# Score products of batches 3 to 7 by row-tiled matmuls, v products pair by pair from batch 4 on, and attention's ranks moved forward, in a block-causal attention and SwiGLU kernel

## Chip, cores and metric

The kernel runs on one core of a Trainium2 chip. The metric is the device time of one launch in microseconds (us), as the median of several runs. Five engines work side by side: TensorE (PE, with its weight loads shown apart as PEld), VectorE (DVE), ScalarE (ACT), GpSimd (POOL) and SyncE (SP, which here issues nearly all DMAs).

## The reference, cut to what matters

```python
# q, k, v: (8 batches, 8 heads, 576 positions, 64), fp32; q and k scaled up by about 4
scores = (1.0 / np.sqrt(64)) * np.matmul(q, k.transpose(0, 1, 3, 2))
mask   = (pos // 64)[:, None] >= (pos // 64)[None, :]          # causal by blocks of 64
scores = np.where(mask, scores, -1e9)
attn   = np.exp(scores - scores.max(-1, keepdims=True))
attn   = attn / (attn.sum(-1, keepdims=True) + 1e-09)
x      = np.matmul(attn, v)                                    # -> (4608 tokens, 512)
g      = x @ w_gate                                            # 512 -> 1536
out    = (g / (1 + np.exp(-g)) * (x @ w_val)) @ w_out          # 1536 -> 512
```

Tokens are numbered batch by batch, so that batch b gives tokens 576 b to 576 b + 575.

## The kernel before, in words

**Precision.** Wherever fp32 accuracy is wanted, an operand is kept as two fp32r parts, "high" (a rounded copy, made by ACT) and "low" (what the copy lost, made by DVE), and a product is made of three: high by high, high by low, low by high.

**Attention.** `attention(...)` (L358) lists the work of one pair of heads of one batch; there are four pairs in a batch, 32 in all. It computes scores transposed (128 keys on the partitions, queries along the row) for the five chunks of keys of a head, only for the queries that may see the chunk, so the chunks are 576, 448, 320, 192 and 64 queries wide. Then: maxima over chunks (DVE, L721) and over partitions (POOL, L725), subtraction (DVE, L749), exponent (ACT, L753), products with v (PE, L831, 28 matmuls for a pair, two heads side by side in the 64-column halves), sums over chunks (DVE, L721 again) and over partitions (POOL, L882), and stores of x and of the sums to DRAM (SP, L900 and L907). There are three ways of making the scores, chosen by batch at L706:

- `plain_scores` (batches 0 and 1): plain fp32 products, L453.
- `split_scores` (batches 3 to 7, 20 pairs): for each head, high and low part of the keys lie one above the other on all 128 partitions, so that two matmuls with 128 rows (L580) make the three products: 24 matmuls for a pair. They come in four groups (two for each head), each with a PSUM buffer `at` of its own, of which there are two. Before them, for q and for k: a load (4 DMAs, L527), a transpose (DVE, L538), three copies in 64-partition halves (ACT, L542; two of them for k) and two subtractions in halves (DVE, L548). Behind them: four copies out of PSUM (ACT, L590) and six small ones that hide the blocks not to be seen (ACT, L600).
- `row_scores` (batch 2, in the set `ROWS`, 4 pairs): the heads lie in the two 64-row halves of the array, and a matmul of 64 rows of one head is issued next to that of the other; three matmuls for a chunk and head (L664), 36 for a pair. They come in four groups too (288 queries, 288 queries, 448 + 64, 320 + 192), each with an `at`. Before them, for q and for k: the same 4 DMAs and transpose (L640), one copy (ACT, L643) and one subtraction (DVE, L646) on 128 partitions. Behind them: four copies out of PSUM (ACT, L681) and three that hide (ACT, L693).

**Products with v.** A pair's generator stops where its products with v are to be made, and is kept in the list `at_work`. `with_v(rank)` (L1248) makes one task of all pairs in the list: of one pair in batches 0 and 1, of two pairs from batch 2 on (one run of 56 matmuls).

**SwiGLU.** `feed_forward(j, ...)` (L1077) does tile j of 256 tokens, 18 tiles. Each has six steps: 24 matmuls for gate and 24 for value (both L1116, PSUM buffers `gv`), tanh (ACT, L1150), two multiplications (DVE, L1153 and L1158), high part (ACT, L1163), low part (DVE, L1166), and 12 matmuls with w_out (L1208, L1209, L1210). In tiles 0 to 3 (`FINE`) these are cut into small tasks; from tile 4 on the 48 matmuls of gate and value follow each other without anything between, and the 12 are one task.

**Order of the work.** All tasks are put in a list with an engine, an estimated cost, a rank, predecessors and buffers. `in_order()` (L1305) plays the engines through with these costs: an engine that comes free takes, among the tasks whose predecessors are done and whose buffers are free, that of lowest rank; PE prefers a task of the same `mode` as the last ("rows" for the 64-row products, "columns" for the products with v). The program is then issued in that order, for every engine and for the queues of SP and POOL. Buffers of `qk`, `parts`, `sc`, `mx`, `v`, `xu`, `gv`, `hhl` and others are handed out in order of creation (`IN_TURN`), and most of them there are two of; a pair from batch 2 on holds one `sc` (scores), one `mx`, one `v` and one `xu`.

The rank of a pair h of batch b is, from batch 2 on, `10 + b - LEAD + h/8`, with corrections `SHIFT` for batches 2 and 3; its scores up to the maxima have a rank lower by `EAGER`. The ranks of SwiGLU's matmuls are `10 + token/576` from tile 2 on (10.89 and up), of its ACT and DVE work 0.5 and a little, of fetching x 1.0 and a little. Pieces of the weights, which are taken apart by ACT and DVE at the beginning, have ranks of -47 to 60. Where the plan leaves PE idle for over 0.3 us, small matmuls on ones (L1425) fill the gap.

Of the kernel before, what the change touches and what calls it, by code (L numbers as in the profile page):

```python
# [18 lines left out]
def kernel(  # L19
# [30 lines left out]
    XT = 256  # L50


    LEAD, EAGER = 6.5924, 0.1229

    SUMS = 2


    ROWS = (2,)
    MIXED = (0, 0, 1, 1, 0, 1, 0, 0, 1, 1, 0, 1)

    FINE = 4
# [296 lines left out]
    def attention(R, b, h, a, e, early, bufs, lane):  # L358
# [346 lines left out]

        (plain_scores if early else row_scores if b in ROWS else split_scores)()  # L706

# [538 lines left out]
    at_work = []  # L1246

    def with_v(rank):  # L1248
        us, products, after, bufs = zip(*(next(pair) for pair in at_work))
        t = add(  # L1250
            "PE", sum(us), rank, lambda: [f() for f in products], sum(after, []), sum(bufs, []), mode="columns"
        )
        for pair in at_work:
            try:
                pair.send(t)
            except StopIteration:
                pass
        at_work.clear()
# [3 lines left out]
    for b in range(B):  # L1262
        for a, e, R in FIRST.get(b, [(0, S, 10.0 + b - LEAD)]):
            early = b in FIRST
            lanes = 2 if e <= half else 1
            for h in range(0, H, 2):
                lane = h // 2 % lanes
                if not lane:
                    if early:
                        bufs = [Buf("qk", "pair"), Buf("parts", "pair")]  # L1270
                    elif b in ROWS:
                        bufs = [(Buf("qk", "raw"), Buf("qk", "keys")), Buf("parts", "queries")]
                    else:
                        bufs = [
                            (Buf("qk", "raw"), Buf("qk", "high")),
                            (Buf("parts", "low0"), Buf("parts", "low1")),
                        ]
                    bufs += [Buf(x) for x in "sc mx v xu".split()]
                    bufs.append(Buf("sr") if b < SUMS else bufs[3])
                rank = R[h // 2] if early else R + h / H + (SHIFT[b][h // 2] if b in SHIFT else 0.0)  # L1280
                at_work.append(attention(rank, b, h, a, e, early, bufs, lane))

                if early or len(at_work) == 2:
                    with_v(rank)
    for i in range(NFC):
        for kind in range(3):
# [174 lines left out]
```

## Time and profile before

| | |
|---|---|
| median of 3 runs | 1163.17 us (1162.48 to 1164.80) |
| span of the profiled execution, first to last instruction (what lies around it isn't listed apart) | 1161.9 us |
| PE busy | 1149.6 us |
| DVE, ACT, POOL busy | 742.4, 620.0, 321.0 us |
| granted TensorE clock, mean | 0.997 |
| bytes moved by DMA | 197.44 MB, mean 170 GB/s |
| first and last matmul of L664 (batch 2) | 205.2 and 271.4 us |
| first and last matmul of L580 (batches 3 to 7) | 303.9 and 903.3 us |

In the lists of the timeline, a row gives the start, the duration, engine, line and operation, what it writes and reads, its shape, and how many equal ones follow each other (x24). Matmuls overlap each other in these durations; what one costs is the distance from its start to the next one's start. A table by stretches gives the busy time of every engine in each stretch, the number of instructions (x), the granted clock as a share (PEclk), and the share and rate of the DMA engines.

### The profile page before, as it was taken

Reading aid. Unit: us, or ns where it says so; the run is one execution under the profiler, and the core shown is the slowest. Engines: PE = TensorE matmul, PEld = TensorE weight load, DVE = VectorE, ACT = ScalarE, POOL = GpSimd, SP = SyncE. Lnnn points to the kernel's source line nnn. Section 1 sums busy time; section 2 is a strip of 40 time slices with the busy share of each in tenths; the row PEclk is TensorE's granted clock in tenths of the full one; section 3 lists DMA queues with packets and bytes.
Section 4 is the critical chain, followed back from the end, with each engine's and each line's share of the span. In section 5 each row is a group of like instructions: output and inputs, shape, how many; then the busy total and the mean of one; then the engine's idle time right before and its main releaser. Section 6 shows DMA issues by size and latency. Waiting matters only on the chain.

```text
span 1161.9 us, 22310 instructions
## 1 busy us (share of the span) xinstructions
PE 1149.6 (99%) x8744; PEld 1032.7 (89%) x8744; DVE 742.4 (64%) x1230; ACT 620.0 (53%) x1114; POOL 321.0 (28%) x141
## 2 busy tenths in 40 slices
PE   8999999999999999999999999999999999999998
PEld 6678788889899989898998989898998989999997
DVE  4998898877697857576774747576575643323222
ACT  5889776745676655473745556473655422212111
POOL 3213101153525263334133423333233420000000
PEclk8999999999999999999999999999999999999999
DMA  8757757776657466663656565663674445444442
GB/s 204 211 158 211 201 190 237 200 206 159 169 149 204 117 188 180 193 152 115 188 169 198 140 185 143 196 166 121 173 201 150 144 144 172 144 164 138 144 170 103
DMA packets 266986, 197.44 MB, mean 170 GB/s; under 512 B 195264, under 2 KB 231376, under 8 KB 266880
## 3 DMA queue, kind: packets, MB, share of 16 engines
q1 hardware_dynamic: 264304, 195.29, 58.0%
q8 instruction: 69, 1.13, 0.4%
q10 hardware_dynamic: 2576, 0.72, 0.3%
q14 instruction: 37, 0.30, 0.1%
HBM read 171.57 MB, written 24.38 MB: 169 GB/s over the span
## 4 chain that ended last, share of the span: by engine, by line
PE 92%; ACT 4%; DMA 2%; DVE 1%; SPq 0%; issue 0%; ACTq 0%
PE gv L1116 50%; PE at L831 8%; PE po L1208 8%; PE po L1210 7%; PE po L1209 7%; PE at L580 6%; PE at L453 1%; PE at L664 1%; PE at L1208 1%; PE at L1209 1%; PE at L1210 1%; ACT sc L471 1%; DMA qk<-in_k_dram 1%; ACT sc L753 1%; PE at L427 0%; ACT ob L970 0%
## 5 line engine op out<-in xcount | busy, mean ns | idle before, releaser
L1116 PE MATMUL gv<-xhl,v_all 128*128 128x256 f32 x2592 | 323.4, 278 | 0.1
L1116 PEld LDWEIGHTS gv<-xhl,v_all 128*128 128x128 f32 x2592 | 308.1, 188 | 4.0 <-issue 1.5
L725 POOL PARTITION_ALL_REDUCE mx<-mx x80 | 140.6, 1805 | 391.5 <-DVE mx L721 138.8
L882 POOL PARTITION_ALL_REDUCE mx<-mx x48 | 178.2, 3765 | 227.0 <-DVE mx L721 213.5
L1153 DVE SCALAR_TENSOR_TENSOR t<-t,gv 128x512 f32<-128x512 f32 x108 | 73.9, 684 | 159.8 <-ACT t L1150 159.1
L1116 PE MATMUL gv<-xhl,g_even 128*128 128x256 f32 x1296 | 173.4, 280 | 0.0
L1116 PEld LDWEIGHTS gv<-xhl,g_even 128*128 128x128 f32 x1296 | 164.2, 188 | 7.0 <-issue 0.8
L1116 PE MATMUL gv<-xhl,g_odd 128*128 128x256 f32 x1296 | 168.9, 277 | 0.0
L1116 PEld LDWEIGHTS gv<-xhl,g_odd 128*128 128x128 f32 x1296 | 157.1, 188 | 1.9 <-issue 1.4
L1163 ACT CAST hhl<-t 128x512 fp32r<-128x512 f32 x108 | 67.2, 622 | 164.3 <-PE po L1209 88.4
L1208 PE MATMUL po<-wo,hhl 128*128 128x512 f32 x372 | 147.5, 397 | 0.0
L1210 PE MATMUL po<-wo,hhl 128*128 128x512 f32 x372 | 145.2, 390 | 0.4 <-DVE hhl L1166 0.4
L1209 PE MATMUL po<-wo,hhl 128*128 128x512 f32 x372 | 145.5, 391 | 0.0
L1166 DVE TENSOR_TENSOR hhl<-t,hhl 128x512 fp32r<-128x512 f32 x108 | 83.3, 773 | 89.5 <-ACT hhl L1163 89.2
L749 DVE TENSOR_TENSOR sc<-sc,mx 128x640 f32<-128x640 f32 (+6 forms) x168 | 122.8, 772 | 16.9 <-POOL mx L725 16.8
L1150 ACT ACTIVATE t<-gv 128x512 f32<-128x512 f32 x108 | 64.6, 598 | 114.9 <-PE gv L1116 109.6
L1158 DVE SCALAR_TENSOR_TENSOR t<-t,gv 128x512 f32<-128x512 f32 x108 | 73.8, 683 | 80.1 <-PE gv L1116 79.2
L753 ACT ACTIVATE sc<-sc 128x1024 f32<-128x1024 f32 (+3 forms) x104 | 105.6, 1031 | 33.7 <-DVE sc L749 33.1
L721 DVE TENSOR_TENSOR mx<-mx,sc 128x128 f32<-128x128 f32 (+2 forms) x180 | 105.0, 588 | 2.2
L590 ACT ACTIVATE sc<-at 128x576 f32<-128x576 f32 x80 | 66.8, 838 | 52.6 <-PE at L580 51.0
L831 PE MATMUL at<-sc,v 128*64 128x320 f32 (+4 forms) x888 | 91.5, 359 | 1.2 <-ACT parts L435 0.9
L831 PEld LDWEIGHTS at<-sc,v 128*64 128x64 f32 x888 | 58.9, 137 | 35.1 <-issue 2.1
(161 smaller groups left out, 1409.2 us busy)
## 6 DMA issues: line engine op xcount, KB each, us to landing
wo<-wo_d SPq DMA_DIRECT2D x200, 512.0 KB
out_dram<-ob SPq DMA_DIRECT2D x35, 256.0 KB
v<-in_v_dram SPq DMA_DIRECT2D x64, 128.0 KB
xt<-x_d SPq DMA_DIRECT2D x64, 128.0 KB
rt<-r_d SPq DMA_DIRECT2D x128, 64.0 KB
qk<-in_q_dram SPq DMA_DIRECT2D x112, 72.0 KB
qk<-in_k_dram SPq DMA_DIRECT2D x104, 72.0 KB
x_d<-xu SPq DMA_DIRECT2D x24, 288.0 KB
```

The costliest lines, as they stand in the source:

```text
L721: nc.vector.tensor_tensor(into, prev, of(c), op)
L725: nc.gpsimd.partition_all_reduce(m, m, channels=P, reduce_op=bass_isa.ReduceOp.max)
L749: nc.vector.tensor_tensor(piece(c), scores_of(c), m, ALU.subtract)
L753: nc.scalar.activation(x, x, AF.Exp)
L831: nc.tensor.matmul(ps[0][own(x), 1 - i if sums else i, q0 - s0 : s1 - s0], lhsT=ones if sums else vt[0][:, 2 * lane + c, own(x)], rhs=sc[0 ...
L882: nc.gpsimd.partition_all_reduce(m, m, channels=P, reduce_op=bass_isa.ReduceOp.add)
L1116: nc.tensor.matmul(o, lhsT=part[:, d], rhs=xs[d][1][x][:, 0:w], start=first, stop=last)
L1153: nc.vector.scalar_tensor_tensor(t[0][:, 0:n], t[0][:, 0:n], 1.0, pg[0][:, 0:n], ALU.add, ALU.mult)
L1166: nc.vector.tensor_tensor(hh[1][:, 0:n], t[0][:, 0:n], hh[0][:, 0:n].bitcast(F32), ALU.subtract)
L1208: nc.tensor.matmul(po, lhsT=hi, rhs=whi, start=i + y == 0, stop=False)
L1209: nc.tensor.matmul(po, lhsT=hi, rhs=wlo, start=False, stop=False)
L1210: nc.tensor.matmul(po, lhsT=lo, rhs=whi, start=False, stop=i + y == NFC - 1)
```

## The change

The ranks of attention from batch 2 on become lower by 3.41 (10.0 instead of 6.5924 is taken off), `EAGER` changes from 0.1229 to 0.1; the scores of batches 3 to 7 are made by `row_scores` instead of `split_scores`; and from batch 4 on `with_v` is called for each pair alone, where batches 2 and 3 keep two pairs together.

```diff
-    LEAD, EAGER = 6.5924, 0.1229
+    LEAD, EAGER = 10.0, 0.1
...
-    ROWS = (2,)
+    ROWS = (2, 3, 4, 5, 6, 7)
...
                 at_work.append(attention(rank, b, h, a, e, early, bufs, lane))

-                if early or len(at_work) == 2:
+                if early or len(at_work) == (2 if b < 4 else 1):
                     with_v(rank)
```

## The prediction

> **What bounds the kernel now.** I read the page first (busy time of the engines), then a table by stretches, then PE's timeline around the runs of attention's matmuls, then the groups of DVE, ACT and POOL.
>
> ```profile
> span 1161.9 us, 22310 instructions
> PE 1149.6 (99%) x8744; PEld 1032.7 (89%) x8744; DVE 742.4 (64%) x1230; ACT 620.0 (53%) x1114; POOL 321.0 (28%) x141
> 200.00:300.00 100.00, 99.64 (x778) 87.97 (x779) 81.44 (x127) 61.92 (x105) 31.68 (x13) 1.00 0.70 192
> 300.00:940.00 640.00, 640.00 (x4808) 585.38 (x4805) 430.12 (x674) 360.35 (x647) 244.62 (x84) 1.00 0.58 165
> 940.00:1162.00 222.00, 218.23 (x1582) 204.28 (x1580) 63.84 (x109) 40.78 (x74) 2.11 (x1) 1.00 0.45 149
> ```
>
> PE is busy for 1149.6 of 1161.9 us, and from 300 to 940 us for all of it, at a clock of 1.00, while DVE has 430 of 640 us, ACT 360, POOL 245. From 300 us on nothing but PE's own work sets the end: SwiGLU's matmuls fill every gap that attention leaves, and attention ends before 940, with 222 us of SwiGLU alone behind it. From 200 to 300 us PE lacks 0.4 us; the 3.8 us missing at the end are the last tile's way out. So the change is worth what it does to the sum of PE's matmuls and of the distances between them. The other engines count only where they would leave PE without work.
>
> **Scores, batches 3 to 7 (20 pairs).** What a matmul costs is the distance between starts. First SwiGLU alone, as a measure; then a pair of batch 2 (`row_scores`), whose four groups go in two visits, with the work before and behind each; then the visits of another pair of it that stayed single.
>
> ```profile
> 958.41 2.88 PE L1116 MATMUL gv<-xhl,v_all 128*128 128x256 f32 x24
> 961.13 0.40 PE L1208 MATMUL po<-wo,hhl 128*128 128x512 f32 x1
> ...
> 265.66 1.18 PE L1116 MATMUL gv<-xhl,g_odd 128*128 128x256 f32 x9
> 266.77 1.06 PE L664 MATMUL at<-parts,qk 64*128 64x288 f32 x12
> 267.76 0.62 PE L1116 MATMUL gv<-xhl,g_odd 128*128 128x256 f32 x3
> 268.22 0.39 PE L1208 MATMUL po<-wo,hhl 128*128 128x512 f32 x1
> ...
> 269.37 0.40 PE L1210 MATMUL po<-wo,hhl 128*128 128x512 f32 x1
> 269.70 1.97 PE L664 MATMUL at<-parts,qk 64*128 64x448 f32 x24
> 271.60 0.50 PE L1208 MATMUL po<-wo,hhl 128*128 128x512 f32 x1
> 271.94 0.40 PE L1209 MATMUL po<-wo,hhl 128*128 128x512 f32 x1
> ...
> 204.74 0.50 PE L1116 MATMUL gv<-xhl,g_even 128*128 128x256 f32 x3
> 205.17 0.67 PE L664 MATMUL at<-parts,qk 64*128 64x288 f32 x6
> 205.76 0.62 PE L1116 MATMUL gv<-xhl,g_even 128*128 128x256 f32 x3
> 206.22 0.87 PE L1116 MATMUL gv<-xhl,v_all 128*128 128x256 f32 x6
> ```
>
> 24 products of L1116 take 961.13 - 958.41 = 2.72, so one takes 0.113 and three take 0.34; one of L1208 to L1210 takes 0.23 where nothing disturbs it (684.33 - 684.10 in the next fence). The visit of 12 (288 and 288 queries) lasts from 266.77 to 267.76, 0.99. The nine products ahead of it take 1.11 instead of 1.02 (+0.09), the three behind it 0.46 instead of 0.34 (+0.12): 1.20 in all. The visit of 24 lasts from 269.70 to 271.60, 1.90; ahead of it L1210 takes 0.33 instead of 0.23 (+0.10), behind it L1208 takes 0.34 (+0.11): 2.11. **A pair in two visits costs 3.31.** Each visit pays some 0.21 for the change into 64-row tiles and back. The price of a visit that breaks up follows from the last four rows: a single group of 288 lasts 0.59 and pays 0.09 and 0.12, 0.80, so two of them 1.60 instead of 1.20, +0.40. The other half pays at least for coming and going once more, +0.21. I take the mean, 0.3; a pair in four visits costs 3.31 + 0.61 = 3.92.
>
> Now `split_scores`, which the change takes away:
>
> ```profile
> 684.10 0.39 PE L1210 MATMUL po<-wo,hhl 128*128 128x512 f32 x1
> 684.33 0.29 PE L580 MATMUL at<-qk,parts 128*128 128x288 f32 x1
> ...
> 685.97 0.41 PE L1208 MATMUL po<-wo,hhl 128*128 128x512 f32 x1
> 686.22 0.39 PE L1209 MATMUL po<-wo,hhl 128*128 128x512 f32 x1
> ...
> 705.72 0.30 PE L580 MATMUL at<-qk,parts 128*128 128x288 f32 x1
> ...
> 707.38 0.41 PE L1208 MATMUL po<-wo,hhl 128*128 128x512 f32 x1
> ...
> L580 PE MATMUL at<-qk,parts x240: 191/292/471, 303.9 to 903.2; 128*128 128x288 f32 x40, 128*128 128x448 f32 x40, 128*128 128x320 f32 x40
> L664 PE MATMUL at<-parts,qk x144: 188/292/469, 205.2 to 271.4; 64*128 64x288 f32 x48, 64*128 64x448 f32 x24, 64*128 64x64 f32 x24, 64*128 64x320 f32 x24
> ```
>
> A run of 12 lasts from 684.33 to 685.97, 1.64, and from 705.72 to 707.38, 1.66. Ahead of it L1210 takes its usual 0.23; behind it L1208 takes 0.25 (+0.02). Full-height matmuls come and go almost without a price. **A pair costs 3.34.** The 240 matmuls of this row, from 303.9 to 903.2, alternate with as many on the low queries; the 480 lie in 44 runs: 36 of 12, four of 4 and four of 8; a broken run costs nothing here. Of the 144 of L664 the first two pairs went in eight visits and the last two in four.
>
> So the new scores have less work inside the visits (0.99 + 1.90 = 2.89 against 3.30) and give nearly all of it back in coming and going, the doors of a visit. In two visits each: 20 x (3.31 - 3.34) = -0.6 us. In four visits each: 20 x (3.92 - 3.34) = +11.6. These are the bounds. I take two visits for all but one half of the 40: from batch 4 on SwiGLU's tasks between two visits are 12 to 48 matmuls long, and between the visits ACT has only two copies of 576 to make where it has 576 and 1024 today, under which 36 of 40 halves held together. That adds one break, +0.3.
>
> The Trainium skill, TensorEngine Tiling (Array Packing), Key Properties, says that changing the tiling mode drains the TensorE, without a figure; the trace agrees, 0.09 to 0.12 us each way. The Trainium skill, same title, Theoretical Speedup, promises up to 2x where the contraction is 64 or less; what that would make stands with the third rival.
>
> The loads stay (4 DMAs for q and 4 for k on SP in both forms), as do the transposes, POOL's work and the number of `at` buffers. ACT and DVE get less work for each pair:
>
> ```profile
> L548 DVE TENSOR_TENSOR parts<-sr,qk 64x576 fp32r<-64x576 f32 x38 | 28.5, 750 | 8.4 <-ACT qk L542 8.0
> L646 DVE TENSOR_TENSOR qk<-sr,qk 128x576 fp32r<-128x576 f32 x4 | 3.0, 750 | 0.0
> L749 DVE TENSOR_TENSOR sc<-sc,mx 128x1152 f32<-128x1152 f32 (+4 forms) x100 | 77.5, 816 | 15.7 <-POOL mx L725 15.7
> ```
>
> DVE makes two subtractions of 0.75 for four, -1.5 a pair; ACT two casts for six and three hiding copies for six. I cost that at nothing: PE hides it, and it is worth at most the 0.4 us that PE lacks from 200 to 300 us.
>
> **Products with v alone, batches 4 to 7 (16 pairs).** Eight visits become 16. What a further visit costs:
>
> ```profile
> 673.10 2.88 PE L1116 MATMUL gv<-xhl,v_all 128*128 128x256 f32 x24
> ...
> 675.91 2.92 PE L831 MATMUL at<-sc,v 128*64 128x256 f32 x28
> ...
> 678.66 2.88 PE L831 MATMUL at<-sc,v 128*64 128x256 f32 x28
> 681.47 0.50 PE L1208 MATMUL po<-wo,hhl 128*128 128x512 f32 x1
> 681.81 0.39 PE L1209 MATMUL po<-wo,hhl 128*128 128x512 f32 x1
> ```
>
> This run of 56 holds two pairs (shown in its halves, from two windows). The 24 products ahead of it take 2.81 instead of 2.72, +0.09. Its first half takes 2.75, its second, which ends in the change back, 2.81, +0.06. L1208 behind it takes 0.34, +0.11. Together 0.26, and 8 x 0.26 = +2.1 us; the other bound is 0, if two pairs come ready so close that the plan puts them side by side. I take +2.1: the pairs come one by one.
>
> Today a couple's first pair waits with its products, and holds its `sc`, `v` and `xu`, until its partner's exponents are done. Alone, it leaves earlier, and the pair after next gets these buffers earlier: attention runs faster and ends well before 940 us. That moves SwiGLU's matmuls, and makes none shorter. In PE's queue the run of 28 waits for one pair's exponents instead of two; what stands behind it is SwiGLU, whose next step the plan puts ahead where the exponents come later.
>
> **Ranks.** All pairs from batch 2 on move by the same 3.41, so their order among themselves stays; `EAGER` moves no pair past another. Buffers go in order of creation, so no pair of batch 2 can pass the last one of batch 1 (rank 29.1), on SP's queue or POOL's either, and the first 200 us stay. On PE, batch 2's first pair (12.88 to 9.47) and batch 3's third (11.87 to 8.46) pass tiles 2 and 3 (10.89 to 11.78); the others were ahead already. On DVE, ACT and SP three pairs pass SwiGLU's 0.5 and the 1.0 of fetching x: batch 2's fourth (1.62 to -1.79) and batch 3's second and fourth. There a block of five subtractions, 5 x 0.816 = 4.1 us, can go ahead of a step's tanh, products or low part. Bounds: 0, and 3 x 4.1 = 12.2 us if PE had nothing else. The nearest row is the stretch from 300 to 940 us, where PE is full beside 430 us of DVE. I take +0.2. Below nothing is excluded but for the 0.4 us that PE lacks there.
>
> **Sum.** -0.6 + 0.3 + 2.1 + 0.2 = +2.0 us on a span of 1161.9: 1163.9. The median of the runs lies 1.27 above that span, so the time is 1163.17 + 2.0 = 1165.2 us. Less than 0.2% (2.3 us) is about what a measurement of this kernel, whose three runs spread over 2.3 us, can't tell from no change.
>
> **Rivals.** (1) *The visits break up*, which ends slower. `at` has two buffers, and a visit of two groups needs both when PE turns to it. Now single v runs, twice as many, hold one at other times than the scores' own. For it: batch 2's first two pairs all went in single groups. Against: its last two didn't, nor did 36 of 40 halves of the split form. It decides from a second and third break on (1.7 + 3 x 0.3 = 2.6, over the 2.3); ten, one in every other pair, give 1163.17 + 1.7 + 3.0 = 1167.9.
>
> (2) *SwiGLU is fed late* by the three pairs that overtake it, or by DVE and POOL in a denser attention. For it: DVE has 81 of 100 us from 200 to 300, where PE lacks 0.4. Against: PE lacks nothing at 67% of DVE later. Half of the 12.2 gives 1163.17 + 1.8 + 6.1 = 1171.1; it decides from 0.5 us on.
>
> (3) *The tiles pay*, which ends faster: if score visits and v visits come side by side, the doors vanish, 20 x (2.89 - 3.34) = -9.0, and with the eight v visits 1163.17 - 9.0 + 2.1 = 1156.3. Against: none of the rows above has such a neighbour. If two heads in half the rows cost one, 36 matmuls would be 18 full ones against 24, 3.30 x 18/24 = 2.48 a pair: 1163.17 + 20 x (2.48 - 3.34) + 2.1 gives 1148.1; the 2.89 measured inside is against it, and it has 0.01 of this rival's chance. The Trainium skill's 2x (TensorEngine Tiling (Array Packing), Theoretical Speedup) is this case.
>
> (4) *The change does less than it says*: the v runs meet and stay in couples. Then 1163.17 - 0.6 + 0.3 + 0.2 = 1163.1.
>
> **How the numbers follow.** The forecast 0.52, of which 0.15 lie over the border of +2.3 us (its own range is 1164 to 1167); rival (1) 0.17, (2) 0.13, (3) 0.12, (4) 0.06. Faster: (3), 0.12. Same: 0.37 + 0.06 = 0.43. Slower: 0.15 + 0.17 + 0.13 = 0.45. The range leaves out most of (3) and the upper part of (1) and (2), some 0.2: 1161.5 to 1169.5.
>
> **What the profile after would show.** L580 gone and 864 matmuls of L664, in 40 to 45 visits from batch 3 on; 16 runs of 28 and four of 56 of L831 from batch 2 on; PE at 100% from 300 us on; DVE busy for some 30 us less (20 x 1.5), ACT for more than that; POOL idle well before 940 us. PE's busy time higher by about 2 us. The prediction is wrong if visits of single groups are common, if PE shows gaps between 200 and 400 us, or if visits of L664 and L831 stand side by side.

## The result, and the profile after

The changed kernel takes 1171.07 us (median; 1169.60 to 1172.78) against 1163.36 of the kernel before in the same series: a ratio of 1.0065 [1.0053, 1.0077], +7.7 us. In a second series (e11 below) it was 1.0046 [1.0032, 1.0060], +6.1 us. It is slower than the 1165.2 forecast and lies above the range of 1161.5 to 1169.5; of the rivals it is (2), SwiGLU fed late, that shows in the trace. The profiled execution took 1169.60 us, its span is 1167.8.

The page of the kernel after, its first two lines of numbers:

```profile
span 1167.8 us, 22687 instructions
PE 1154.6 (99%) x9024; PEld 1024.6 (88%) x9024; DVE 714.4 (61%) x1186; ACT 549.0 (47%) x974; POOL 316.3 (27%) x141
```

The table by stretches of the kernel after (PE, PEld, DVE, ACT, POOL busy; PEclk; share and rate of DMA):

```profile
200.00:300.00 100.00, 99.18 (x755) 87.88 (x754) 72.27 (x116) 56.95 (x98) 32.26 (x13) 1.00 0.66 184
300.00:940.00 640.00, 639.68 (x5068) 570.99 (x5067) 411.01 (x644) 292.22 (x512) 241.53 (x84) 1.00 0.56 165
940.00:1167.00 227.00, 224.16 (x1619) 209.60 (x1618) 64.06 (x104) 42.23 (x76) 0.00 (x0) 1.00 0.42 147
```

DVE lost 28.0 us of work, ACT 71.0, and PE still shows 639.68 of 640 us. The clock is 1.00. Read only so, the table says that PE is as full as before and has 5.0 us more to do. That is half of the truth, as two rows about the filling matmuls on ones (L1425) show. They hold all matmuls of that line on the buffer `at`; the numbers behind the count are the shortest, median and longest duration in ns and the starts of the first and the last. First the kernel before, then the kernel after:

```profile
L1425 PE MATMUL at<-ones x74: 222/238/369, 1.0 to 12.6; 128*64 128x64 f32 x74
```

```profile
L1425 PE MATMUL at<-ones x114: 222/222/367, 1.0 to 350.5; 128*64 128x64 f32 x114
```

Before, the last one on `at` starts at 12.6 us. After, there are 40 more, up to 350.5 us: stretches where PE has nothing to do, and which the column "busy" counts as work.

**A budget of distances.** To see all of it I sorted PE's distances from start to start, between the 577th matmul of L1116 (two tiles have 576 of them; it starts at 217 to 220 us in each kernel) and the first one of the last tile's last step. In that stretch all kernels have the same 4560 matmuls of L1116 and 1140 of L1208 to L1210. A SwiGLU matmul counts 0.113 or 0.228 us; what is above it next to a visit of attention is that visit's door; fillers, and what else is above by 0.04 us or more, are gaps; the remainder is spread thinly. In us:

| kernel | total | scores and doors | products with v and doors | gaps | spread thinly |
|---|---|---|---|---|---|
| before | 929.3 | 77.7 | 69.1 | 0.8 | 6.5 |
| after (e11: the same to 0.1) | 936.1 | 77.6 | 71.4 | 4.6 | 7.2 |
| e1, ranks alone | 950.5 | 78.7 | 68.9 | 20.9 | 6.8 |
| e2, scores alone | 931.2 | 76.4 | 69.2 | 2.0 | 8.4 |
| e3, v alone | 931.8 | 78.3 | 71.4 | 0.8 | 6.2 |
| e4, all but the ranks | 933.3 | 77.0 | 71.6 | 2.0 | 7.4 |
| e5, three pairs back | 934.4 | 77.0 | 71.6 | 2.9 | 7.7 |
| e6, the other five back | 934.8 | 77.5 | 71.5 | 2.9 | 7.7 |
| e7, no late fillers | 935.6 | 77.6 | 71.6 | 3.3 | 7.9 |
| e8, v in couples | 933.4 | 76.9 | 69.0 | 4.3 | 8.0 |
| e9, side work first | 933.3 | 77.1 | 71.6 | 2.1 | 7.3 |
| e10, batch 3 in split form | 929.8 | 76.8 | 69.1 | 0.7 | 8.0 |
| e12, e2 without late fillers | 930.2 | 76.4 | 69.1 | 0.6 | 8.9 |

The change in one line: scores -0.1, v +2.3, gaps +3.8, thinly +0.7, together +6.8 (the parts are rounded). The spans differ by only 5.9, because this stretch starts 0.8 us earlier in the trace after. That is no more than chance gives: in five traces with the same order up to there (after, e1, e5, e7, e11) it starts anywhere from 217.0 to 218.7 us.

**Where the gaps are.** The kernel before has one of over 0.5 us, 0.65 at 281 us. The kernel after has them in three places. The two smaller ones, 0.60 and 0.72 us, are waits of PE for ACT's copy of the output out of PSUM (L1235). In ACT's queue the first of these copies stands behind a cast that waits for DVE (L1163), the second behind exponents of 1.17 us (L753):

```profile
231.12 0.50 PE L1208 MATMUL at<-wo,hhl 128*128 128x512 f32 x1 [0.32 <-ACT ob L1235]
...
296.84 0.50 PE L1208 MATMUL po<-wo,hhl 128*128 128x512 f32 x1 [0.45 <-ACT ob L1235]
```

The largest, 2.8 us with its edges, lies between 345 and 350.5 us. PE's timeline of the kernel after (start, us, engine, line, operation, tiles, shape, count):

```profile
343.83 1.30 PE L1116 MATMUL gv<-xhl,v_all 128*128 128x256 f32 x10
345.06 1.38 PE L1425 MATMUL at<-ones 128*64 128x64 f32 x20
346.36 0.50 PE L1208 MATMUL po<-wo,hhl 128*128 128x512 f32 x1
...
349.00 0.39 PE L1210 MATMUL po<-wo,hhl 128*128 128x512 f32 x1
349.31 1.32 PE L1425 MATMUL at<-ones 128*64 128x64 f32 x19
350.42 0.43 PE L831 MATMUL at<-sc,v 128*64 128x256 f32 x1
...
362.08 1.08 PE L1116 MATMUL gv<-xhl,g_even 128*128 128x256 f32 x7
```

From 345.06 to 346.36 and from 349.31 to 350.42 PE multiplies ones: 2.4 us. DVE of the kernel after, around the first of these, and then what it does for tile 4's x (division L1068, low part L350, two of four pieces each):

```profile
341.28 4.49 DVE L749 TENSOR_TENSOR sc<-sc,mx 128x640 f32<-128x640 f32 x6
345.69 0.68 DVE L1166 TENSOR_TENSOR hhl<-t,hhl 128x512 fp32r<-128x512 f32 x1
...
353.97 0.76 DVE L1068 TENSOR_TENSOR xt<-xt,rt 128x256 f32<-128x256 f32 x2
...
361.71 0.76 DVE L350 TENSOR_TENSOR xhl<-xt,xhl 128x256 fp32r<-128x256 f32 x2 [6.78 <-ACT xhl L347]
```

The same work on ACT of the kernel after:

```profile
340.39 0.62 ACT L1163 CAST hhl<-t 128x512 fp32r<-128x512 f32 x1 [1.05 <-DVE t L1158]
...
356.16 1.31 ACT L848 COPY xu<-at 128x256 f32<-128x256 f32 x4 [4.86 <-PE at L831]
...
361.25 0.72 ACT L347 CAST xhl<-xt 128x256 fp32r<-128x256 f32 x2
```

The high part of a SwiGLU step is there at 341.0 (340.39 + 0.62). Its low part needs 0.68 us, but starts at 345.69, behind a block of six subtractions of scores, 4.49 us. PE's products with w_out (346.36) wait for just that. At 349.31 PE could go on with tile 4 or with the next v run. The exponents of the latter come only then, and tile 4's x is late: divided at 354.7, cast only at 361.25, because ACT's queue has the copies out of the v products (L848), of the next scores (L681) and of the output (L1235) ahead of it, and those wait for PE. The first product of tile 4 starts at 362.08, 0.4 us after the third low part began, directly behind a score visit. Before, it was otherwise (DVE, then PE of the kernel before):

```profile
339.41 1.35 DVE L749 TENSOR_TENSOR sc<-sc,mx 128x1152 f32<-128x1152 f32 x1
...
341.61 2.02 DVE L749 TENSOR_TENSOR sc<-sc,mx 128x896 f32<-128x896 f32 x3
...
346.80 0.42 DVE L1068 TENSOR_TENSOR xt<-xt,rt 128x256 f32<-128x256 f32 x1
...
348.97 0.42 DVE L350 TENSOR_TENSOR xhl<-xt,xhl 128x256 fp32r<-128x256 f32 x1
```

```profile
353.00 1.57 PE L1116 MATMUL gv<-xhl,g_even 128*128 128x256 f32 x12
```

There DVE's subtractions came in smaller lots with x's pieces between, the last low part was done at 349.4, and tile 4's first product started 3.6 us later. In the kernel after, the last low part is done at 362.5, 13.1 us later: more than that slack.

### The profile page after: what moved, and what is told of

Its sections match the earlier page's. It is cut to its first block, busy times and chain, and to the rows that moved or that the text cites. A ratio compares the mean times of both kernels' runs of the same rounds, so it can differ in the third digit from the quotient of the medians.

```text
span 1167.8 us, 22687 instructions
## 1 busy us (share of the span) xinstructions
PE 1154.6 (99%) x9024; PEld 1024.6 (88%) x9024; DVE 714.4 (61%) x1186; ACT 549.0 (47%) x974; POOL 316.3 (27%) x141
## 4 chain that ended last, share of the span: by engine, by line
PE 93%; ACT 4%; DMA 1%; DVE 1%; issue 0%; SPq 0%
PE gv L1116 50%; PE po L1208 8%; PE at L831 8%; PE po L1209 7%; PE po L1210 7%; PE at L664 6%; PE at L453 1%; ACT sc L753 1%; PE at L1208 1%; PE at L1209 1%; PE at L1210 1%; ACT sc L471 1%; DMA qk<-in_k_dram 1%; PE at L427 1%; DMA qk<-in_q_dram 1%; ACT ob L1235 0%
## 5 line engine op out<-in xcount | busy, mean ns | idle before, releaser
L1116 PE MATMUL gv<-xhl,v_all 128*128 128x256 f32 x2592 | 322.1, 277 | 0.1
L1116 PEld LDWEIGHTS gv<-xhl,v_all 128*128 128x128 f32 x2592 | 307.5, 188 | 3.3 <-issue 1.2
L882 POOL PARTITION_ALL_REDUCE mx<-mx x48 | 177.7, 3752 | 240.4 <-DVE mx L721 215.4
L725 POOL PARTITION_ALL_REDUCE mx<-mx x80 | 136.7, 1756 | 297.6 <-DVE mx L721 189.1
L1153 DVE SCALAR_TENSOR_TENSOR t<-t,gv 128x512 f32<-128x512 f32 x108 | 74.1, 686 | 173.8 <-ACT t L1150 173.3
L1116 PE MATMUL gv<-xhl,g_even 128*128 128x256 f32 x1296 | 175.5, 281 | 0.0
L1116 PEld LDWEIGHTS gv<-xhl,g_even 128*128 128x128 f32 x1296 | 164.8, 188 | 9.3 <-issue 1.6
L1116 PE MATMUL gv<-xhl,g_odd 128*128 128x256 f32 x1296 | 170.0, 278 | 0.0
L1163 ACT CAST hhl<-t 128x512 fp32r<-128x512 f32 x108 | 67.0, 621 | 203.0 <-PE po L1209 117.6
L1116 PEld LDWEIGHTS gv<-xhl,g_odd 128*128 128x128 f32 x1296 | 157.7, 188 | 2.4 <-issue 1.5
L1208 PE MATMUL po<-wo,hhl 128*128 128x512 f32 x372 | 150.6, 405 | 0.5 <-ACT ob L1235 0.5
L1210 PE MATMUL po<-wo,hhl 128*128 128x512 f32 x372 | 145.1, 390 | 0.0
L1166 DVE TENSOR_TENSOR hhl<-t,hhl 128x512 fp32r<-128x512 f32 x108 | 87.2, 809 | 94.3 <-ACT hhl L1163 94.3
L1158 DVE SCALAR_TENSOR_TENSOR t<-t,gv 128x512 f32<-128x512 f32 x108 | 74.0, 685 | 98.5 <-PE gv L1116 97.9
L753 ACT ACTIVATE sc<-sc 128x1024 f32<-128x1024 f32 (+3 forms) x104 | 105.4, 1032 | 33.0 <-DVE sc L749 32.3
L721 DVE TENSOR_TENSOR mx<-mx,sc 128x128 f32<-128x128 f32 (+2 forms) x180 | 102.1, 577 | 2.6 <-ACT sc L693 0.9
L681 ACT ACTIVATE sc<-at 128x576 f32<-128x576 f32 (+1 forms) x96 | 78.6, 839 | 52.3 <-PE at L664 51.4
L831 PE MATMUL at<-sc,v 128*64 128x320 f32 (+4 forms) x888 | 94.1, 361 | 0.7 <-ACT sc L693 0.3
L831 PEld LDWEIGHTS at<-sc,v 128*64 128x64 f32 x888 | 61.3, 137 | 34.1 <-issue 1.4
```

Source lines behind the costliest of these rows:

```text
L681: nc.scalar.mul(sc[0][:, :, o0 : o0 + gw], ps[0][:, :, 0:gw], SCALE)
L721: nc.vector.tensor_tensor(into, prev, of(c), op)
L725: nc.gpsimd.partition_all_reduce(m, m, channels=P, reduce_op=bass_isa.ReduceOp.max)
L753: nc.scalar.activation(x, x, AF.Exp)
L831: nc.tensor.matmul(ps[0][own(x), 1 - i if sums else i, q0 - s0 : s1 - s0], lhsT=ones if sums else vt[0][:, 2 * lane + c, own(x)], rhs=sc[0 ...
L882: nc.gpsimd.partition_all_reduce(m, m, channels=P, reduce_op=bass_isa.ReduceOp.add)
```

## The experiments

Each kernel was timed beside the kernel before (medians of 1163.8 to 1164.1 us). The first four take the change apart.

**e1, the ranks alone**, on the kernel before:

```diff
-    LEAD, EAGER = 6.5924, 0.1229
+    LEAD, EAGER = 10.0, 0.1
```

> The kernel before with only LEAD and EAGER changed (scores split, v products in couples). Theory A, late x: the ranks of batches 2 and 3 alone make batch 2 finish late, and PE runs dry ahead of tile 4. The list that these ranks give has 111 filling matmuls more, all around the first products of tile 4, which at the kernel's own 0.107 us and FILL of 0.6 stands for a planned gap of 20 us. So 1175 to 1184 us, with the gap ahead of tile 4. Theory B, the visits: ranks cost nothing, all of the 7.7 us come from the doors of score and v visits, so 1162 to 1165 us. The prediction's term for the ranks was +0.2 us.

Measured: 1184.51 us, ratio 1.0178 [1.0164, 1.0192], +20.7. No other part costs nearly as much, and it is far over the bound of 12.2. The gaps hold 20 of the 21 us. PE of e1, the three places of its late fillers, 8 + 34 + 180 of them:

```profile
341.49 0.68 PE L1425 MATMUL at<-ones 128*64 128x64 f32 x8
...
347.95 2.20 PE L1425 MATMUL at<-ones 128*64 128x64 f32 x34
...
361.22 10.66 PE L1425 MATMUL gv<-ones 128*64 128x64 f32 x180
```

DVE of e1 beside the last of them:

```profile
362.17 2.38 DVE L1068 TENSOR_TENSOR xt<-xt,rt 128x256 f32<-128x256 f32 x2 [0.63 <-DMA xt<-x_d]
364.58 3.76 DVE L548 TENSOR_TENSOR parts<-sr,parts 64x576 fp32r<-64x576 f32 x2
368.37 0.76 DVE L350 TENSOR_TENSOR xhl<-xt,xhl 128x256 fp32r<-128x256 f32 x2
```

PE multiplies ones for 10.6 us, while tile 4's x waits for its division, and its low part waits behind the subtractions with which `split_scores` takes q and k apart (L548). The low part is done at 369.1, and the fillers, whose number the plan sets, run on to 371.8; so not all of the 10.6 us need be waiting. Another 2.9 us of the gaps is a wait of PE behind it, at 380.6, which ends with a multiplication on DVE (L1153).

**e2, the scores alone**, on the kernel before:

```diff
-    ROWS = (2,)
+    ROWS = (2, 3, 4, 5, 6, 7)
```

> The kernel before with only ROWS changed (score products of batches 3 to 7 in 64-row halves), ranks and couples as before. Both theories can count this one from the distances in the trace after: 664 has 70.5 us of its own and 57 visits of 0.20, 81.7 in all, where before L664 and L580 had 81.8 with their doors. Theory A: no change from the visits (-1 to +1) and up to 1.6 us from the 9 filling matmuls that the list has between the fourth and fifth tile, 1163 to 1165.5. Theory B: half of the loss or more sits here, 1167 to 1170.

Measured: 1165.62 us, 1.0018 [1.0009, 1.0027], +2.1. The score products themselves are 1.3 us cheaper. Gaps take 1.2 of that back, and 1.9 us more are spread over SwiGLU's matmuls. The two gaps are rows of PE in e2:

```profile
293.17 0.80 PE L1425 MATMUL at<-ones 128*64 128x64 f32 x10
...
323.24 0.68 PE L1425 MATMUL at<-ones 128*64 128x64 f32 x8
```

**e3, the v products alone**, on the kernel before:

```diff
-                if early or len(at_work) == 2:
+                if early or len(at_work) == (2 if b < 4 else 1):
```

> The kernel before with only the products with v of batches 4 to 7 made pair by pair. Theory A: eight more visits at 0.26 to 0.30 us, +2.1 to +2.4, so 1165.3 to 1166. The list has no filling matmuls more than before. Theory B: the doors cost more than the distances show, 1167 to 1171. If single visits cost nothing: 1163.4.

Measured: 1167.12 us, 1.0027 [1.0016, 1.0038], +3.2 (1.9 to 4.4); by the distances +2.5, of which +2.3 are the visits. A run of one pair with its neighbours, from PE's timeline of the kernel after:

```profile
605.26 2.88 PE L1116 MATMUL gv<-xhl,v_all 128*128 128x256 f32 x24
608.08 2.92 PE L831 MATMUL at<-sc,v 128*64 128x256 f32 x28
610.93 0.50 PE L1208 MATMUL po<-wo,hhl 128*128 128x512 f32 x1
611.27 0.39 PE L1209 MATMUL po<-wo,hhl 128*128 128x512 f32 x1
```

Ahead +0.10 (2.82 instead of 2.72), in itself +0.10 (2.85 instead of 2.75), behind +0.11 (0.34 instead of 0.23): 0.31, and eight more runs of it 2.5 us.

**e4, everything but the ranks**: the kernel after with the old first line.

```diff
-    LEAD, EAGER = 10.0, 0.1
+    LEAD, EAGER = 6.5924, 0.1229
```

> The changed kernel with LEAD and EAGER as before. Theory A: what remains is the sum of the two visits' terms, -0.1 and +2.3, and 0 to 1.6 us of gaps: 1165 to 1167.5, so that over half of the 7.7 us comes back. PE is full at the start of tile 4. Theory B: as the changed kernel, 1170 to 1172.

Measured: 1167.90 us, 1.0034 [1.0021, 1.0046], +3.9. So the ranks, +20.7 alone, cost only 1.4 to 3.6 us on top of the other two (the kernel after at 1.0046 and 1.0065 less e4, whose own interval is 1.4 us to each side), 2.8 by the distances. The parts don't add up: 2.1 + 3.2 + 20.7 = 26.0 against 6.1 to 7.7. The large gap of e1, 10.66 us at tile 4, is not in the kernel after. What differs there is the form of the scores of batch 3, above all its preparation, with half the subtractions on DVE and a third of the casts on ACT. The single v runs have no part in it: e8 below is e2 with the new ranks, v in couples in both, and the ranks cost 2.2 us there (933.4 less 931.2). So the form of the scores decides what the ranks cost; that it is the lighter preparation is what e1's rows say, but no kernel changed the preparation by itself.

**e5 and e6: which pairs?** In the kernel after, e5 puts three pairs (batch 2's fourth, batch 3's second and fourth) back to their old ranks; e6 puts back the five others of batches 2 and 3 and leaves those three moved.

```diff
# e5
-    SHIFT = {2: (7.4686, 5.1562, 10.9114, -4.5382), 3: (1.9556, -4.9491, 4.9621, -5.9019)}
+    SHIFT = {2: (7.4686, 5.1562, 10.9114, -1.1306), 3: (1.9556, -1.5415, 4.9621, -2.4943)}
# e6
+    SHIFT = {2: (10.8762, 8.5638, 14.319, -4.5382), 3: (5.3632, -4.9491, 8.3697, -5.9019)}
```

> The changed kernel, but the three pairs that its ranks move ahead of SwiGLU's ACT and DVE work (batch 2's fourth, batch 3's second and fourth) have their ranks of before; all others stay moved. Theory A1, overtaking: those three ranks are what makes batch 2 late. Then the maxima of batch 2's third pair on POOL start near 270 us again instead of 278, PE isn't short ahead of tile 4, and the time is that of the kernel without the rank change, 1167 to 1169 us. Theory A2, the passing of tiles 2 and 3 on PE by batch 2's first and batch 3's third pair does it: nothing comes back, 1170.5 to 1172.5.

> The counterpart: of batches 2 and 3 only those three pairs keep their new ranks, the other five have those of before. A1: as late as the changed kernel, 1170 to 1173 us, with a gap ahead of tile 4 (its list has 23 filling matmuls there, 4 us planned). A2: 1167 to 1169.

Measured: e5 1169.27 us, 1.0039 [1.0027, 1.0051]; e6 1170.44 us, 1.0050 [1.0038, 1.0062]. The intervals overlap, so the times don't tell them apart. The traces do, for the place: in e5 no filler stands between 331.1 and 365.5 us, and the gap ahead of tile 4, which starts at 351.30 there, is gone; in e6, with three pairs moved alone, a gap of the same size stands ahead of tile 4, though at 358 us, ahead of a score visit, and not at 345. PE, and then DVE, of e6:

```profile
358.20 2.90 PE L1425 MATMUL at<-ones 128*64 128x64 f32 x46
```

```profile
360.29 0.75 DVE L350 TENSOR_TENSOR xhl<-xt,xhl 128x256 fp32r<-128x256 f32 x2
```

So the three pairs that overtake SwiGLU are enough to make a gap of this size there; that the same instruction ends it is not shown. But e5 has new gaps elsewhere, 2.9 us in all, so that taking the three back is worth only 1.7 us of distances. The wait at 231 us for the copy of the output is in e5 as well and not in e6: it comes with the other five pairs.

All pairs together also do something else, earlier. POOL's maxima of batch 2's third pair, in the kernel before, and then in the kernel after:

```profile
270.51 3.91 POOL L725 PARTITION_ALL_REDUCE mx<-mx  x2 [7.20 <-issue]
```

```profile
278.16 8.49 POOL L725 PARTITION_ALL_REDUCE mx<-mx  x4 [14.50 <-ACT hhl L1163]
```

After, they start 7.6 us later, four in a row: as I read DVE's rows, the fourth pair's first maximum went ahead on DVE and waited 3.07 us for its scores. In e5 and e6 the first two start at 270.37 and 271.55, as before. So neither group of pairs alone makes this lateness, and by e6 a gap ahead of tile 4 doesn't need it.

**e7, no fillers behind 100 us**, in the kernel after, to see whether the fillers themselves cost the time:

```diff
-            if t.engine == "PE" and t.gap > 0.3:
+            if t.engine == "PE" and t.gap > 0.3 and t.at < 100.0:
```

> The changed kernel without the small filling matmuls after 100 us (40 of them, 2.5 us of PE around 345 to 350 us). If the gap is real, PE waits there as long as it filled before and the time stays within 1 us of 1171.4. If the filling itself pushed work back, 2 to 2.5 us come back: 1169.

Measured: 1169.68 us, 1.0046 [1.0034, 1.0058], not to be told from the kernel after (1.0046 and 1.0065). By the distances 0.5 us less. The starvation now shows as a wait, with its reason. PE of e7:

```profile
346.91 0.40 PE L1209 MATMUL po<-wo,hhl 128*128 128x512 f32 x1
348.13 0.50 PE L1210 MATMUL po<-wo,hhl 128*128 128x512 f32 x1 [0.82 <-DVE hhl L1166]
...
352.76 3.90 PE L831 MATMUL at<-sc,v 128*64 128x320 f32 x40 [0.15 <-ACT sc L753]
```

A distance of 1.22 instead of 0.23 us, ended by L1166, the low part behind the six subtractions: here the fillers hid a real wait. Of the second gap, 1.3 us with its edges, only 0.33 us is left, ended by the exponents; the rest of it was the fillers' own time. Together 1.4 of the 2.8 us are waits. Still the total is only 0.5 us less, as 0.7 us more is spread thinly here; why is open.

**e8, the kernel after with v in couples.** The label doesn't fit what the kernel is; its fillers are kept.

```diff
-                if early or len(at_work) == (2 if b < 4 else 1):
+                if early or len(at_work) == 2:
```

> The changed kernel with the products with v in couples as before (scores in rows, ranks moved). If the single visits cost what the distances say, 2.1 to 2.4 us come back: 1168.5 to 1169.5. If in this kernel they cost nothing, because SwiGLU waits for x all the same: 1171 to 1172. If the couples starve it more, over 1172.

Measured: 1167.91 us, 1.0029 [1.0019, 1.0038]. The v products fall back by 2.4 us to their old sum, the total by 2.7: single v runs cost the same in this kernel as in e3.

**e9, side work first.** In the kernel after, SwiGLU's ACT and DVE work (0.5 before) and the fetch of x (1.0 before) get ranks that no pair can overtake.

```diff
-        R = 1.0 + j / 1000.0
+        R = -5.0 + j / 1000.0
...
-        E = 0.5 + j / 1000.0
+        E = -5.5 + j / 1000.0
```

> The changed kernel with all of its attention ranks, but SwiGLU's ACT and DVE work at -5.5 instead of 0.5 and the fetching of x at -5.0 instead of 1.0, below the lowest rank of attention (-2.25), so that nothing overtakes them. If overtaking is the cause (A1): the fourth low part of tile 4's x comes before 356 us instead of 362, the gap ahead of tile 4 closes, and the time is that of the kernel with rows and single v runs at the old ranks, 1.003 to 1.004 of the kernel before, 1167 to 1168.5. If the order among the attention pairs or on PE is the cause (A2): as the changed kernel, 1.0065, 1170 to 1172.

Measured: 1168.92 us, 1.0038 [1.0025, 1.0050]. At the place it did what it should; the low parts, DVE of e9:

```profile
344.32 0.67 DVE L1166 TENSOR_TENSOR hhl<-t,hhl 128x512 fp32r<-128x512 f32 x1
...
347.40 0.41 DVE L350 TENSOR_TENSOR xhl<-xt,xhl 128x256 fp32r<-128x256 f32 x1
```

x is there 14 us earlier than in the kernel after, no filler stands at 345 or 349, and the distances are 933.3 in sum, those of e4. But their stretch starts at 219.2 instead of 217.0, and that takes most of it back. It is more than chance: from PE's 1201st matmul to the start of the stretch it takes 71.8 us, against 69.6 to 69.9 in the five traces named above. Ten fillers more stand there, six at 167.7 and four at 195.7 us, and PE waits for pieces of the weights behind the latter:

```profile
195.70 0.45 PE L1425 MATMUL at<-ones 128*64 128x64 f32 x4
196.39 0.50 PE L1116 MATMUL gv<-xhl,g_odd 128*128 128x256 f32 x2 [0.24 <-ACT g_odd L989]
```

In time, e9 (1.0038) can't be told from the kernel after beside it (1.0046, e11).

**e10, scores without batch 3**, on the kernel before:

```diff
-    ROWS = (2,)
+    ROWS = (2, 4, 5, 6, 7)
```

> The kernel before with rows in batches 4 to 7 alone (16 pairs; batch 3 stays split, ranks and couples as before). Its list has no filling matmuls, so the visits stand alone. By the distances (a pair of two visits 3.31, split 3.34) the scores are worth -0.5 to -1.5 us: 1162.5 to 1164. If the rows cost something that the distances don't show (2.1 us in the kernel with rows in batches 3 to 7, of which 1.3 were filling matmuls): 1164.5 to 1166. If it is below 1162.8, it beats both kernels.

Measured: 1164.61 us, 1.0003 [0.9995, 1.0012]: no difference from the kernel before. The gaps of e2 are gone: they come from making batch 3's scores in rows.

**e11, the kernel after once more**, unchanged:

> The changed kernel itself, next to the other two on the same chip, as their measure: 1.0065 of the kernel before, 1170 to 1172. The fourth low part of tile 4's x at 362 us.

Measured: 1170.01 us, 1.0046 [1.0032, 1.0060]. Its distances agree with the first trace to 0.1 us in each column.

**e12, e2 without fillers behind 100 us** (the edits of e2 and e7 on the kernel before):

> The kernel before with rows in batches 3 to 7 (ranks and couples as before), without the 18 small filling matmuls at 293 and 323 us, which held PE for 1.3 us. If they stood in for a real gap, PE waits as long and the ratio stays that of the kernel with them, 1.0018 (1165 to 1166). If they pushed work back: 1.3 us come back, 1164 to 1164.8, as in the kernel with rows from batch 4 on alone (1.0003).

Measured: 1165.24 us, 1.0008 [0.9999, 1.0017]. Beside e2 (1.0018) the intervals overlap; by the distances up to 1.0 us of e2's loss was its fillers: of the 1.8 us at 293 and 323 us 0.35 are left without them. No kernel of these beat the kernel before.

## Why the prediction was wrong, step by step

**The bound: right.** PE's distances set the time; with 28 us less work on DVE and 71 less on ACT the kernel became slower. The other engines count where they leave PE without work, as the prediction says; in the kernel after there are such places.

**Scores: right in sum.** Forecast -0.6 + 0.3, measured -0.1 in the kernel after and -1.3 in e2. From batch 3 on there are 45 visits, at the upper end of the 40 to 45. Rival (1) did not come.

**v: right.** Forecast +2.1; +2.3 in the budget, +2.5 by the row of one run, +3.2 [1.9, 4.4] for e3. The runs are 16 of 28 and four of 56; rival (4) is out. Rival (3) too: where a score visit stands directly behind a v run, as in the following rows of PE in the kernel after, one door of 0.1 us goes, and there are four such places. The prediction had named such neighbours as a sign that it is wrong; they are there, and worth some 0.4 us in all.

```profile
583.13 2.93 PE L831 MATMUL at<-sc,v 128*64 128x256 f32 x28
585.99 1.13 PE L664 MATMUL at<-parts,qk 64*128 64x448 f32 x12
587.05 0.50 PE L1208 MATMUL po<-wo,hhl 128*128 128x512 f32 x1
587.38 0.39 PE L1209 MATMUL po<-wo,hhl 128*128 128x512 f32 x1
```

The Trainium skill, TensorEngine Tiling (Array Packing), Key Properties, has a drain at every change of the tiling mode; the doors of 0.09 to 0.12 us agree with that. The up to 2x of the Trainium skill, same title, Theoretical Speedup, does not show against a form that fills all 128 rows already: with their doors, the row-tiled scores of the kernel after cost what the full-height ones cost (77.6 against 77.7).

**Ranks: the step that failed.** "The nearest row is the stretch from 300 to 940 us, where PE is full beside 430 us of DVE. I take +0.2." It measured +2.8 by distances in the changed kernel (936.1 against e4's 933.3) and +20.7 alone. The mechanism was named rightly: "a block of five subtractions ... can go ahead of a step's tanh, products or low part", and it was six, 4.49 us, ahead of L1166. The row chosen to weigh it was wrong: an average over 640 us says nothing of the one place where the three pairs cross SwiGLU's next steps, a low part at 345 us and tile 4's x, which had 3.6 us of slack. In the changed kernel the cost lies inside the bounds of 0 and 12.2. With the ranks alone it does not: the bound counted the subtractions, and not that a late x queues behind other work on ACT and DVE (e1: 10.66 us at one spot). That rival (2) had 1171.1 and 1171.07 was measured is chance: its price was 6.1 us, and the gaps are 3.8 more.

**"I cost that at nothing": wrong beside the moved ranks.** The lighter work on ACT and DVE was put at no more than 0.4 us. With the split form the ranks cost 21.2 us by distances (950.5 less 929.3), with the row form 2.2 (e8 less e2). The row form gained nothing over the kernel before, but beside the moved ranks it is worth some 19 us. That this is its lighter work is argued from e1's rows; no kernel changed that work alone.

**Not foreseen.** The gaps that the scores make with the old ranks (+1.2 in e2 and e4; gone in e10), the waits for the copy of the output, and 0.7 us spread over 5700 SwiGLU matmuls, up to 2.4 where rows are used (e12). The last is open: at most 0.3 us of it stands on the second matmul behind a row visit, the rest has no place. The two gaps of e2 and e4, at 293 and 323 us, are not in the kernel after; those at 231 and 296 us are, and they come with the ranks: e1, with no other part of the change, has both, and e2 and e4 have neither.

**"PE at 100% from 300 us on": right by the number, and no evidence.** The 639.68 of 640 holds 40 fillers. "PE shows gaps between 200 and 400 us" was named as what would make the prediction wrong. They were there, most of them as matmuls on ones.

**Ranks of later batches.** That `EAGER` and the move of batches 4 to 7 do nothing holds: with the ranks of batches 2 and 3 alone moved back, the plan of the kernel after is that of e4, task for task; this is read from the two plans, no such kernel was run.

The sum of the steps, by taking kernels from each other: scores -0.1, v +2.3, gaps 1.2 without the ranks (e4) and 2.6 more with them (together 3.8), thinly 0.7, makes +6.8 before rounding; forecast was +2.0. By place all of the larger gaps of the kernel after are the ranks': 2.8 us at 345 to 350.5 and 1.3 at 231 and 296. Open stays how the 2.8 divide between the overtaken work of SwiGLU and the late third pair of batch 2: in time, e5, e6, e9 and the kernel after can't be told apart.

## What to carry to other kernels

Where an order is moved, look for the one place where the moved work crosses something that the bounding engine will soon need, and measure the slack there (the producer's end against the consumer's start); an average over a long stretch hides it. Before trusting a full engine, take out of its busy time the work that only fills gaps, and run the kernel once without it: in the largest gap here half was a wait, and half the filling itself. Parts of a change that share an engine don't add up: time each alone and each left out.

## What was not expected of the hardware

A DVE instruction that starts while POOL runs a reduction over partitions can take several times its usual time. From the kernel before, POOL and then DVE:

```profile
360.09 7.17 POOL L882 PARTITION_ALL_REDUCE mx<-mx  x2 [1.68 <-DVE mx L721]
```

```profile
360.19 2.71 DVE L350 TENSOR_TENSOR xhl<-xt,xhl 128x256 fp32r<-128x256 f32 x1 [0.26 <-ACT xhl L347]
...
364.77 1.97 DVE L1166 TENSOR_TENSOR hhl<-t,hhl 128x512 fp32r<-128x512 f32 x1
```

2.71 us for an instruction that takes 0.42 at 348.97, and 1.97 for one that takes 0.69 elsewhere. There is an order in it. All seven of L1166 in this trace that start 0.7 to 2.2 us into a reduction of L882 end 3.1 us after the reduction began (3.07 to 3.15), however early they started. L1153 and L1158, which read one operand from PSUM (`gv`) where L1166 reads none, take their usual 0.69 us inside the same reductions, ten of the ten that start in the first 1.5 us. This reads as if certain DVE instructions are held up to a fixed point of the reduction; no run here changed an operand to show why. In e1's gap two of L548 took 3.76 us beside such a reduction, where two take 1.54 at 327.98 us in the same kernel.
